# Attention scores in transposed form: 64x32 array tiles and VectorE's block transposes in place of TensorE's

## The chip, the cores and the metric

The kernel runs on one core of a Trainium2 chip. The metric is device time in microseconds (us), the median of several executions; lower is better. The core's engines work from queues of their own, each in program order: TensorE (PE, matmuls and transposes into PSUM), VectorE (DVE), ScalarE (ACT), GpSimd (POOL) and SyncE (SP), which issues most transfers.

## The reference

Three layers follow one another. The change is in the first, an attention whose 576 keys are first pooled into 32 memory slots a head (4 batches, 8 heads, 576 tokens, head size 64):

```python
a = softmax(phi)                      # over the 576 tokens, for each of 32 slots
k_m = einsum('bhsm,bhsd->bhmd', a, k) # 32 x 64 a head
v_m = einsum('bhsm,bhsd->bhmd', a, v)
scores = q @ k_m.T / sqrt(64)         # 576 x 32 a head
attn = softmax(scores)                # over the 32 slots
out = attn @ v_m                      # 576 x 64 a head
```

Its output, 2304 tokens by 512, goes through an ELU MLP (512 to 2048 to 512), and that through a mixture of 8 experts (512 to 1024 to 512, the best 2 of 8 for each token).

## The kernel before, in words

**Main loop.** Work is cut into units: four MLP blocks, one a batch of the attention in order (4, 5, 4, 5 tiles of 128 tokens, 16 steps each), then expert units of 8 steps. The loop (L914) runs over all steps; `i` counts them, so block 0 is i = 0 to 15, block 1 is 16 to 31, block 2 is 32 to 47. Each step issues, in this order: the top tick, a split of weights (`prep_hi` on ScalarE), the first layer (L781, two halves of 288 tokens in block units), the middle tick, the second half of the split, the ELU (ScalarE's two activations, L786 and L787, then VectorE's L794 and L795), in block 0 the conversion of packed weights (`conv1_hi`, `conv1_lo` on ScalarE, `conv2` on VectorE), the late tick, and the second layer of step i - 2 (L826 in block 0, L828 to L830 later). The first layer writes two PSUM banks `ph`, which come free when L795 has read them. So the first layer of step i + 1 follows VectorE's ELU of step i.

**Attention.** `attention(b)` (L139) is a generator. Batch 0 is run straight through before the loop, with an order written out by hand and filler matmuls (`warm`). Batches 1, 2 and 3 are put into blocks 0, 1 and 2: each `yield` names the kind of slot in which the next piece may run ("pe", "light", "gap"), and `tick` (L511) takes pieces at the top, in the middle and late in a step. By these rules the pieces of scores and softmax fall into i = 10 to 13 for batch 1, 25 to 29 for batch 2 and 39 to 43 for batch 3. The first layer of block b reads the result, `xt`, as a rounded high half and a low half (`th`, `tl`); the pooled values `vT` are multiplied into that layer's weights beforehand (`fold`, `fold_half`).

**Scores and softmax.** The pooled keys lie in `kmT`, 128 partitions (two heads, g = 0 and 1, of 64) by four pairs of heads, block-diagonal with zeros. `scores(k)` takes a group of two, two or one token chunks of 128 (the last of 64): a matmul a chunk and pair of heads (L256), whose stationary operand is the chunk of q, puts the tokens on partitions and 32 slots for each of 8 heads on the columns. VectorE takes the maximum over the slots (L269) and subtracts it (L270), out of PSUM; ScalarE takes the exponential (`grow`, L275); VectorE sums, adds 1e-9, inverts and multiplies (`normalize`, L281 to L285; for batch 0 GpSimd multiplies). `turn(k)` transposes back on TensorE (L292), into PSUM; ScalarE copies the rounded high half (L136) and VectorE subtracts for the low half (L137).

**PSUM.** Side work takes banks in turn from those that the second layer leaves free: `px`, and `acc4` too where the block has four tiles. In block 1 (five tiles) `px` is alone (`single()`), and the next piece waits until the last one's data have been read out.

## Time and profile before

| | |
|---|---|
| median of 3 runs | 922.81 us (922.67 to 923.54) |
| span of the profiled execution | 921.2 us |
| around the span, against the median | 1.6 us |
| busy: TensorE, VectorE, ScalarE, GpSimd | 885.3, 539.8, 441.1, 163.8 us |
| mean granted TensorE clock | 0.993 of full speed |
| attention of batch 0 | 0 to 28.3 us |
| block 0, with attention of batch 1 | 28.3 to 133.0 us |
| block 1, with batch 2 | 133.0 to 240.7 us |
| block 2, with batch 3 | 240.7 to 331.8 us |

The profile is of one execution and shows its span; the runs' times hold what lies around it too. Busy times are sums over the span; matmuls overlap one another and their ends are modelled. [...] In a timeline, brackets name the idle time before an instruction and what ended it.

### The profile page before, as it was taken

What the parts mean: (1) busy time and instruction counts of PE and PEld (TensorE: products, weight loads), DVE (VectorE), ACT (ScalarE), POOL (GpSimd) and SP (SyncE); (2) the same over time, 40 slices, a digit from 0 to 9 for tenths busy, and PEclk for the clock granted to TensorE, in tenths of its full rate; (3) what the DMA queues carried; (4) which work ended last, traced back from release to release, by engine and by line L of the source; (5) the groups of instructions that cost most, each with busy time, mean ns of one, the idle gap of its engine ahead of it and who ended that gap; (6) DMA issues with size and microseconds to landing.
All of it is one profiled execution on the core that took longest, in us unless ns stands there. A gap on an engine that the chain in (4) does not pass through costs nothing. (4 is left out here: it accounts for less than half of the span.)

```text
span 921.2 us, 15374 instructions
## 1 busy us (share of the span) xinstructions
PE 885.3 (96%) x5909; PEld 726.2 (79%) x5913; DVE 539.8 (59%) x1164; ACT 441.1 (48%) x967; POOL 163.8 (18%) x246
## 2 busy tenths in 40 slices
PE   8999899999999899999999999999999999999995
PEld 5556457777878777777888888898898998989884
DVE  4876877566687687458667564554544543443421
ACT  4776556445564655555546454443543343332310
POOL 1100000000000404210416412304404032030303
PEclk9999999999999999999999999999999999999998
DMA  9986568655652325441666966647647245162404
GB/s 344 398 292 234 178 229 307 199 200 160 241 180 92 93 92 139 138 138 58 182 153 155 264 206 193 165 133 223 162 155 180 82 97 163 46 147 92 57 1 57
DMA packets 67885, 152.62 MB, mean 166 GB/s; under 512 B 11106, under 2 KB 24162, under 8 KB 66786
## 3 DMA queue, kind: packets, MB, share of 16 engines
q1 hardware_dynamic: 57826, 131.13, 43.2%
q0 software_dynamic: 9984, 20.49, 11.8%
q8 instruction: 47, 0.77, 0.3%
q14 instruction: 28, 0.23, 0.1%
HBM read 119.16 MB, written 32.44 MB: 165 GB/s over the span
## 5 line engine op out<-in xcount | busy, mean ns | idle before, releaser
L828 PE MATMUL acc<-bh,gl 128*128 128x512 f32 (+1 forms) x544 | 217.5, 400 | 1.8 <-DVE rows L849 1.8
L830 PE MATMUL acc<-bh,gh 128*128 128x512 f32 (+1 forms) x544 | 213.7, 393 | 0.0
L829 PE MATMUL acc<-bl,gh 128*128 128x512 f32 (+1 forms) x544 | 213.5, 392 | 0.0
L809 DVE SCALAR_TENSOR_TENSOR gl<-ph,gh 128x312 fp32r<-128x312 f32 (+2 forms) x128 | 61.8, 483 | 217.9 <-ACT gh L808 217.9
L494 ACT ACTIVATE bh<-raw 128x512 fp32r<-128x512 f32 x144 | 90.1, 626 | 77.7 <-PE acc L830 77.6
L830 PEld LDWEIGHTS acc<-bh,gh 128*128 128x128 f32 (+1 forms) x544 | 101.4, 186 | 23.6
L828 PEld LDWEIGHTS acc<-bh,gl 128*128 128x128 f32 (+1 forms) x544 | 101.7, 187 | 19.8 <-DVE rows L849 2.2
L851 POOL DMA_INDIRECT out<-rows,ids x40 | 64.9, 1622 | 292.3 <-DVE rows L849 264.3
L829 PEld LDWEIGHTS acc<-bl,gh 128*128 128x128 f32 (+1 forms) x544 | 101.7, 187 | 18.0
L808 ACT ACTIVATE gh<-ph 128x312 fp32r<-128x312 f32 (+2 forms) x128 | 55.2, 431 | 124.5 <-PE ph L781 123.7
L500 DVE TENSOR_TENSOR bl<-raw,bh 128x512 fp32r<-128x512 f32 x144 | 98.8, 686 | 3.4 <-ACT bh L494 3.4
L781 PE MATMUL ph<-xl,ah 128*128 128x312 f32 (+2 forms) x512 | 96.9, 311 | 0.0
L781 PE MATMUL ph<-xh,ah 128*128 128x312 f32 (+2 forms) x512 | 94.3, 306 | 0.0
L781 PE MATMUL ph<-xh,al 128*128 128x312 f32 (+2 forms) x512 | 94.2, 306 | 0.0
L781 PEld LDWEIGHTS ph<-xl,ah 128*128 128x128 f32 x512 | 81.5, 188 | 6.5
L781 PEld LDWEIGHTS ph<-xh,al 128*128 128x128 f32 x512 | 79.4, 188 | 0.0
L781 PEld LDWEIGHTS ph<-xh,ah 128*128 128x128 f32 x512 | 79.4, 188 | 0.0
L781 PE MATMUL ph<-tl,fh 128*128 128x288 f32 x256 | 64.3, 332 | 4.9 <-DVE elu L795 4.6
L500 DVE TENSOR_TENSOR al<-raw,ah 128x512 fp32r<-128x512 f32 x96 | 65.6, 683 | 0.0
L781 PEld LDWEIGHTS ph<-tl,fh 128*128 128x128 f32 x256 | 41.1, 189 | 30.8 <-issue 14.3
L794 DVE SCALAR_TENSOR_TENSOR elu<-elu 128x288 f32<-128x288 f32 x128 | 57.8, 451 | 11.6 <-ACT elu L787 11.2
L801 ACT ACTIVATE gh<-elu 128x576 fp32r<-128x576 f32 (+1 forms) x48 | 31.8, 663 | 66.0 <-DVE elu L795 66.0
(214 smaller groups left out, 1247.4 us busy)
## 6 DMA issues: line engine op xcount, KB each, us to landing
raw<-in_wmoe SPq DMA_DIRECT2D x48, 1024.0 KB, 5.1
raw<-in_wmlp SPq DMA_DIRECT2D x32, 512.0 KB, 6.2
raw<-wxa SPq DMA_DIRECT2D x12, 1024.0 KB, 6.0
raw<-wxb SPq DMA_DIRECT2D x12, 1024.0 KB, 8.2
kv<-in_kv SPq DMA_DIRECT2D x8, 1024.0 KB, 10.6
out<-zrow SPq DMA_DIRECT2D x13, 512.0 KB, 9.1
q<-in_q SPq DMA_DIRECT2D x8, 576.0 KB, 7.5
x2d<-rows SPq DMA_DIRECT2D x18, 256.0 KB, 3.9
```

What stands on the lines that cost most here:

```text
L494: act.activation(ready[h, c][0], raws[h, c], AF.Copy)
L500: dve.tensor_tensor(lo, raws.pop((h, c)), hi.bitcast(F32), op=OP.subtract)
L781: pe.matmul(ph, w, x, start=k == 0, stop=k == len(terms) - 1)
L794: dve.scalar_tensor_tensor(m, t[:, 0, o], 1.0, m, op0=OP.add, op1=OP.mult)
L801: act.activation(gh[:, o], m, AF.Copy)
L808: act.activation(gh[:, o], ph, AF.Relu)
L809: dve.scalar_tensor_tensor(gl[:, o], ph, 0.0, gh[:, o].bitcast(F32), op0=OP.max, op1=OP.subtract)
L828: pe.matmul(acc, gl[:, o], wh, start=f == 0, stop=False)
L829: pe.matmul(acc, gh[:, o], wl, start=False, stop=False)
L830: pe.matmul(acc, gh[:, o], wh, start=False, stop=f == u["nf"] - 1)
L851: d = pool.indirect_dma_start(out=out, out_offset=bass.IndirectOffsetOnAxis(ap=ids[:m, t, 0:1], axis=0), in_=r, in_offset=None, compute_op ...
```

## The change

`kmT` keeps both heads g on the two halves of the partitions, without zeros, as one copy. `scores(h)` takes half of the tokens (288) and swaps the operands: `kmT` is the stationary operand, 64 rows by 32 columns, q the moving one. Four pairs of heads go to four column tiles and the two g to two row tiles, and the scores come out with 4 x 32 slots on partitions and 288 tokens on columns, one bank for each g. VectorE transposes 32x32 blocks out of PSUM into SBUF, which puts 32 tokens of a block on partitions and the slots on columns; maximum, subtraction, exponential and normalization then run over 128x288 pieces, one for each (h, g). A second block transpose on VectorE gives the layout of `xt`, ScalarE copies the high half from it, and `lower` subtracts the low half, one piece later in the order. Groups of three become quarters of four. In batch 0 the second half of the scores comes behind `fold_half(0)`, and `pooled([1])` ahead of the conversion; in batches 1 to 3 the kinds of slots change with the pieces.

```diff
--- before.py
+++ after.py
@@ -20,6 +20,7 @@
 
 P = 128
 NB, NH, S, HD, NM = 4, 8, 576, 64, 32
+H = S // 2
 N = NB * S
 DM, FF = 512, 2048
 NE, FE = 8, 1024
@@ -116,8 +117,7 @@
                 + [lambda h=h: load_q(b, h) for h in range(2)])
 
 
-    kmT = ap_.tile([P, 4, 2, NM], F32, tag="kmT", name="kmT")
-    dve.memset(kmT, 0.0)
+    kmT = ap_.tile([P, 4, NM], F32, tag="kmT", name="kmT")
     deferred, place = [], [""]
 
     def later(f):
@@ -215,9 +215,7 @@
 
             def put():
                 if 0 in ws:
-                    for g in range(2):
-                        o = slice(64 * g, 64 * g + 64)
-                        act.activation(kmT[o, :, g], bk[o, :P].rearrange("p (j m) -> p j m", m=NM), AF.Copy)
+                    act.activation(kmT.rearrange("p j m -> p (j m)"), bk[:, :P], AF.Copy)
                 if 1 in ws:
                     act.activation(vT, bk[:, P:2 * P], AF.Copy)
 
@@ -242,89 +240,80 @@
         yield
         qt = att["q", b]
         xt = att["x", b] = [fp.tile([P, 2, S], F32R, tag=n, name=n) for n in ("th", "tl")]
-        groups = [(0, 2, P), (2, 2, P), (4, 1, 64)]
         sbs = {}
 
-        def scores(k):
-            c0, k_, n = groups[k]
-            m = k_ * 8
-            bk = side_bank()
-            for i in range(k_):
-                s0 = SCH[c0 + i][0]
-                for p in range(4):
-
-                    pe.matmul(bk[:n, i * 256:(i + 1) * 256].rearrange("t (g j m) -> t j g m", g=2, j=4)[:, p],
-                              qt[:, p, s0:s0 + n], kmT[:, p], start=True, stop=True)
-            sc = bk[:n, :m * NM].rearrange("p (a b) -> p a b", b=NM)
-            mx = sm.tile([P, 16], F32, tag="smx", name="smx", bufs=2)
-            if k < 2:
-                sb = ap_.tile([P, 16, NM], F32, tag="sb", name="sb", bufs=2)
-            elif first:
-                sb = rp.tile([P, DM], F32, tag="rows", name="rows").rearrange("p (a b) -> p a b", b=NM)
-            else:
-                sb = aT[:, 0].rearrange("p a (b c) -> p (a b) c", c=NM)
-            sbs[k] = sb[:n, :m]
-
-            def shift():
-                dve.tensor_reduce(out=mx[:n, :m], in_=sc, axis=AX, op=OP.max)
-                dve.tensor_tensor(sbs[k], sc, mx[:n, :m, None].to_broadcast([n, m, NM]), op=OP.subtract)
-
-            later(shift)
-
-        def grow(k):
-            act.activation(sbs[k], sbs[k], AF.Exp, scale=0.125)
-
-        def normalize(k):
-            c0, k_, n = groups[k]
-            m, sb = k_ * 8, sbs[k]
-            su = sm.tile([P, 16], F32, tag="ssu", name="ssu", bufs=2)
-            dve.tensor_reduce(out=su[:n, :m], in_=sb, axis=AX, op=OP.add)
-            dve.tensor_scalar(su[:n, :m], su[:n, :m], 1e-9, None, op0=OP.add)
-            dve.reciprocal(su[:n, :m], su[:n, :m])
+        def scores(h, gs=(0, 1)):
+            bks = {g: side_bank()[:, :H] for g in gs}
+            for j in range(4):
+                for g in gs:
+                    o, r = slice(64 * g, 64 * g + 64), slice(32 * j, 32 * j + 32)
+                    pe.matmul(bks[g][r], kmT[o, j], qt[o, j, h * H:(h + 1) * H], start=True, stop=True,
+                              tile_position=(64 * g, 32 * j))
+
+            def shift(g):
+                sb = sbs[h, g] = ap_.tile([P, H // 32, NM], F32, tag="sb", name="sb", bufs=4)
+                mx = sm.tile([P, H // 32], F32, tag="smx", name="smx", bufs=2)
+                dve.transpose(sb.rearrange("p a b -> p (a b)"), bks[g])
+                dve.tensor_reduce(out=mx, in_=sb, axis=AX, op=OP.max)
+                dve.tensor_tensor(sb, sb, mx[:, :, None].to_broadcast([P, H // 32, NM]), op=OP.subtract)
+
+            for g in gs:
+                later(lambda g=g: shift(g))
+
+        def grow(h, g):
+            act.activation(sbs[h, g], sbs[h, g], AF.Exp, scale=0.125)
+
+        def normalize(h, g):
+            sb = sbs[h, g]
+            su = sm.tile([P, H // 32], F32, tag="ssu", name="ssu", bufs=2)
+            dve.tensor_reduce(out=su, in_=sb, axis=AX, op=OP.add)
+            dve.tensor_scalar(su, su, 1e-9, None, op0=OP.add)
+            dve.reciprocal(su, su)
             eng = pool if first else dve
-            eng.tensor_tensor(sb, sb, su[:n, :m, None].to_broadcast([n, m, NM]), op=OP.mult)
-
-        def turn(k):
-            c0, k_, n = groups[k]
-            bk = side_bank()
-            for i in range(k_):
-                for g in range(2):
-                    pe.transpose(bk[:, (i * 2 + g) * P:(i * 2 + g) * P + n],
-                                 sbs[k][:, i * 8 + g * 4:i * 8 + g * 4 + 4].rearrange("p a b -> p (a b)"),
-                                 ident[:n, :n])
-            s0 = SCH[c0][0]
-            src = bk[:, :k_ * 2 * P].rearrange("p (i g n) -> p g i n", i=k_, g=2)[:, :, :, :n]
-            later(lambda: halve(src, *(t[:, :, s0:s0 + k_ * n].rearrange("p g (i n) -> p g i n", i=k_)
-                                       for t in xt)))
+            eng.tensor_tensor(sb, sb, su[:, :, None].to_broadcast([P, H // 32, NM]), op=OP.mult)
+
+        def turn(h, g):
+            back = sbs[h, g, "back"] = ap_.tile([P, H], F32, tag="back", name="back", bufs=2)
+            dve.transpose(back, sbs[h, g].rearrange("p a b -> p (a b)"))
+            act.activation(xt[0][:, g, h * H:(h + 1) * H], back, AF.Copy)
+
+        def lower(h, g):
+            hi, lo = (t[:, g, h * H:(h + 1) * H] for t in xt)
+            dve.tensor_tensor(lo, sbs[h, g, "back"], hi.bitcast(F32), op=OP.subtract)
 
         if first:
             scores(0)
-            grow(0)
-            scores(1)
-            grow(1)
+            grow(0, 0)
+            grow(0, 1)
             warm(6)
+            pooled([1])
             conv2([("a", 0), ("a", 1)])
             load_to(3)
             keep([("a", 0), ("a", 1)])
             load_phi(1)
-            normalize(0)
-            pooled([1])
-            scores(2)
+            normalize(0, 0)
+            normalize(0, 1)
             conv1_hi(pieces(0))
-            grow(2)
             warm(6)
-            normalize(1)
             across([1])
+            turn(0, 0)
+            turn(0, 1)
+            lower(0, 0)
+            lower(0, 1)
             conv1_lo(pieces(0))
             warm(4)
-            turn(0)
-            normalize(2)
-            warm(2)
             fold_half(0)
             warm(2)
-            turn(1)
+            scores(1)
+            grow(1, 0)
+            grow(1, 1)
             warm(2)
-            turn(2)
+            normalize(1, 0)
+            normalize(1, 1)
+            turn(1, 0)
+            turn(1, 1)
+            lower(1, 0)
+            lower(1, 1)
             conv2(pieces(0))
             conv1_hi(pieces(1))
             conv1_lo(pieces(1))
@@ -332,29 +321,29 @@
                 f()
         else:
             yield "gap"
-            scores(0)
-            if single():
-                yield
-            scores(1)
+            for h in range(2):
+                if single():
+                    scores(h, [0])
+                    yield
+                    scores(h, [1])
+                else:
+                    scores(h)
+                yield "light"
+                grow(h, 0)
+                grow(h, 1)
+                if h == 0:
+                    yield
+            held = None
+            for h in range(2):
+                for g in range(2):
+                    yield "light"
+                    if held:
+                        lower(*held)
+                    normalize(h, g)
+                    turn(h, g)
+                    held = h, g
             yield "light"
-            grow(0)
-            grow(1)
-            yield
-            scores(2)
-            yield "light"
-            normalize(0)
-            grow(2)
-            yield "light"
-            normalize(1)
-            yield "gap" if b == 3 else "pe"
-            turn(0)
-            if single():
-                yield
-            turn(1)
-            yield "light"
-            normalize(2)
-            yield "gap"
-            turn(2)
+            lower(1, 1)
 
     def warm(n):
 
```

## Rows read from the trace of the kernel before

**Rows 1.** Page, first part: busy us (share of the span) and instructions of each engine.

```profile
PE 885.3 (96%) x5909; PEld 726.2 (79%) x5913; DVE 539.8 (59%) x1164; ACT 441.1 (48%) x967; POOL 163.8 (18%) x246
```

**Rows 2.** Windows in block 0 (us; busy us and instructions by engine; clock; DMA).

```profile
76.23:80.93 4.70, 4.70 (x23) 3.03 (x22) 3.73 (x6) 3.44 (x10) 0.00 (x0) 1.00 0.58 182
80.93:86.74 5.81, 5.81 (x38) 3.32 (x37) 4.30 (x9) 4.58 (x10) 0.00 (x0) 1.00 0.90 324
102.87:114.32 11.45, 7.96 (x31) 4.81 (x29) 9.92 (x18) 5.47 (x11) 0.00 (x0) 0.85 0.54 174
86.74:128.22 41.48, 36.87 (x201) 22.43 (x199) 33.44 (x57) 21.87 (x45) 0.00 (x0) 0.96 0.51 164
```

**Rows 3.** Waits of TensorE over the span: us in total, times, longest.

```profile
PE acc L292 <- DVE sb L285: 2.3, 1, 2.3
PE px L567 <- DVE tl L137: 2.0, 2, 1.0
```

**Rows 4.** Windows, end of block 3; the last columns are clock, DMA share, GB/s.

```profile
430.00:434.00 4.00, 4.00 (x16) 3.52 (x16) 3.21 (x8) 3.59 (x9) 0.00 (x0) 0.57 0.18 23
```

**Rows 5.** Windows in block 1: i = 23, and i = 24 to 30.

```profile
178.33:183.44 5.11, 5.11 (x31) 4.51 (x28) 3.75 (x8) 2.94 (x7) 0.00 (x0) 1.00 0.69 177
183.44:235.14 51.70, 48.83 (x376) 38.13 (x374) 33.72 (x76) 24.43 (x62) 0.00 (x0) 1.00 0.51 166
```

**Rows 6.** Windows in block 2: i = 40, and i = 39 to 43.

```profile
289.38:293.84 4.46, 4.46 (x26) 3.78 (x25) 3.44 (x8) 3.54 (x9) 0.00 (x0) 1.00 0.68 227
280.65:314.05 33.40, 30.95 (x236) 25.64 (x229) 27.23 (x61) 17.64 (x46) 4.19 (x10) 1.00 0.35 97
```

**Rows 7.** Groups by line, shapes apart: busy us, mean ns of one, idle before.

```profile
L256 PE MATMUL px<-kmT,q 128*128 128x64 f32 x64 | 7.7, 273 | 0.0
L794 DVE SCALAR_TENSOR_TENSOR elu<-elu 128x288 f32<-128x288 f32 x128 | 57.8, 451 | 11.6 <-ACT elu L787 11.2
L270 DVE TENSOR_TENSOR sb<-px,smx 128x512 f32<-128x512 f32 x4 | 2.8, 692 | 0.1
L285 POOL TENSOR_TENSOR sb<-sb,ssu 128x512 f32<-128x512 f32 x2 | 2.1, 1048 | 20.7 <-DVE ssu L283 20.7
```

**Rows 8.** Timeline of VectorE in block 2: start us, us, instruction.

```profile
306.74 0.40 DVE L281 TENSOR_REDUCE ssu<-aT 64x8 f32<-64x256 f32 x1
307.17 0.16 DVE L282 TENSOR_SCALAR ssu<-ssu 64x8 f32<-64x8 f32 x1
307.37 0.19 DVE L283 RECIPROCAL ssu<-ssu 64x8 f32<-64x8 f32 x1
307.60 0.42 DVE L285 TENSOR_TENSOR aT<-aT,ssu 64x256 f32<-64x256 f32 x1
307.94 0.17 DVE L671 TENSOR_TENSOR g_pr<-g_o,g_pos 128x32 f32<-128x32 f32 x1
```

**Rows 9.** Timeline of TensorE in blocks 1 and 3 (matmuls; idle before in brackets).

```profile
205.67 1.06 PE L419 MATMUL px<-raw,vT 64*32 64x512 f32 x8
206.66 0.53 PE L781 MATMUL ph<-tl,fh 128*128 128x288 f32 x2
...
429.33 0.54 PE L781 MATMUL ph<-tl,fh 128*128 128x288 f32 x2 [1.83 <-DVE elu L795]
```

**Rows 10.** Timeline of the start, all engines.

```profile
13.86 3.34 PE L256 MATMUL acc<-kmT,q 128*128 128x64 f32 x28 [0.19 <-DMA q<-in_q]
...
18.57 1.22 DVE L465 SCALAR_TENSOR_TENSOR cv<-cvm,cvl 128x1024 int32<-128x1024 int32 x1
...
23.86 1.24 ACT L457 ACTIVATE cvl<-raw,top 128x1024 int32<-128x1024 uint16 x1
...
28.32 0.54 PE L781 MATMUL ph<-tl,fh 128*128 128x288 f32 x2
...
31.31 0.46 DVE L794 SCALAR_TENSOR_TENSOR elu<-elu 128x288 f32<-128x288 f32 x1
...
32.31 0.53 PE L781 MATMUL ph<-tl,fh 128*128 128x288 f32 x2
```

## The prediction

> **What bounds the kernel now.** I read the page first: TensorE is busy for 96% of the span and no other engine for 60% [rows 1]. So work taken from TensorE is worth its time only where nothing else is late, and the windows by stretch say where that is. I cut the trace at the starts of the first layer (L781), one cut per iteration i of the main loop. In block 0 an iteration without attention work takes 4.70 us, and 5.81 us with a half fold in it, and VectorE is busy for 3.73 and 4.30 us of these [rows 2]: it has about a quarter to spare. While the softmax of batch 1 runs (i = 10 to 14) the same iterations take 41.48 us, and i = 12 alone 11.45 us, of which VectorE is busy for 9.92 [rows 2]. The list of waits shows the reason: TensorE stood 2.3 us in front of its transposes (L292) for VectorE's normalization (L285) [rows 3]. Block 1 runs at 5.11 us an iteration when undisturbed, with 3.75 us of VectorE, block 2 at 4.46 us with 3.44 [rows 5, 6]. The attention of batches 1, 2 and 3 is slipped into blocks 0, 1 and 2; that of batch 0 stands alone at the start. So the change acts in four places, and in three of them VectorE is nearly as full as TensorE. I sum up over the four.
>
> **What the pieces cost.** *TensorE, removed.* A batch has 20 score matmuls, two records each; 64 records of the full size cover 7.7 us, 0.12 us each [rows 7]. With the short last group that is 4.5 us a batch. Ten transposes at about the same pace add 1.2.
>
> *TensorE, added.* Sixteen matmuls of 64x32 tiles by 288 columns, eight for each half. The nearest rows are folds, which use the same tiles. Behind layer 1, a half fold of 256 columns lengthens an iteration by 5.81 - 4.70 = 1.1 us [rows 2]; at the top of an iteration a single-g fold of 512 columns takes 1.0 us from its start to the next layer 1 [rows 9], and 288 columns instead of 512 leave about 0.65. Both g together cost what one costs, since their tiles run side by side. So batches 1 and 3 pay about 1.1 + 0.65 each, batch 2, with one bank to itself and four separate sets, 0.65 + 3 x 1.1 = 3.95.
>
> *VectorE.* A 128x288 operation takes 0.45 us [rows 7]. In a chain, one that needs the last starts 0.43 us after a 0.40 us one, and one that doesn't starts 0.34 us after a 0.42 us one [rows 8]. For 288 columns I take 0.49 and 0.37. The four steps of a normalization start 0.43, 0.20, 0.23 and 0.34 apart at 256 columns [rows 8]. The block transpose isn't in the trace. Its bounds are the 256-wide reduction, 0.40 us [rows 8], and the 512-wide subtraction, 0.69 us [rows 7]; I take 0.48, nearest to the 288-wide row. [...]
> So one (h, g) quarter costs 1.34 us for transpose, maximum and subtraction, 1.75 for normalization and transpose back, 0.37 for the low half: 3.5 us, 14 a batch. Before, by the same spacings, it is 3.5 for the shifts, 4.8 for the normalizations, 1.5 for the low halves: 9.8. VectorE gets about 4.2 us more a batch.
>
> *ScalarE.* Four exponentials and four high halves of 288 columns against three and three wider ones: equal. But the high half (L136 before) is now issued right behind VectorE's transpose and ahead of ScalarE's elu activations of that iteration, so these now wait for VectorE's normalization too. The memset of kmT goes (once), and kmT takes one copy instead of two: 0.3 us at the start, not on the path, since the second load of q arrives at 13.86 us [rows 10].
>
> **Batch 0, at the start.** Scores of the first half are out at 14.5 us (q's arrival at 13.86, then two waves of tiles). VectorE: shifts to 17.4, the scale of the moved pooled([1]) at 18.2 (it follows that step's matmuls, estimate 1.8 us behind warm(6)), the two conversions to 20.7 (18.57 before [rows 10]), normalizations of both g to 22.4, GpSimd's products (0.66 us for 288 columns, from 1.05 for 512 [rows 7]) to 23.1, transposes, low halves to 24.5. The fold's halves wait for ScalarE's 1.24 us conversion (L457, at 23.86 before [rows 10]) and end at 26.3. Only then come the second half's shifts, behind them in VectorE's queue: 2.7 us, normalizations 1.9, the product 0.66, transpose, copy and low half 1.3: 32.8 us. Layer 1 of i = 0 starts its first half early (26.4, against 28.32 [rows 10]), but its second half needs these values and TensorE stands for about 5.7 us. Conversions of 2.4 us follow on VectorE before the elu (L794), which starts at 35.3 where it started at 31.31, so layer 1 of i = 1 goes from 32.31 [rows 10] to 36.3: 4.0 us lost. [...] Loss: 5.2.
>
> **Batch 1, i = 10 to 14 (41.48 us [rows 2]).** Times from layer 1 of i = 10. Both shifts (2.7 us) stand in front of elu: layer 1 of i = 11 at 6.6. In i = 11 the half fold needs the two banks of the second scores, and these come free only when VectorE has finished two conversions (2.5 us) and both transposes: TensorE stands 2.3 us, layer 1 of i = 12 at 15.4. At the top of i = 12 a normalization holds elu back: 21.2. Then a full VectorE turn: elu, two conversions, low half, normalization, transpose (end 26.6), the high half on ScalarE, low half, normalization, transpose (29.2), ScalarE's high half, elu: layer 1 of i = 13 ends at 22.9, that of i = 14 can't start before 31.1, that of i = 15 not before 39.4. Gain 2.1, less 0.7 in i = 15, whose elu waits for the conversions: 1.4. A low clock hides behind VectorE here.
>
> **Batch 2, i = 24 to 30 (51.70 us [rows 5]).** Seven times 5.11 is 35.8, four single folds 4.0, five gating pieces of four short instructions at 0.45 (pace of [rows 7]) 2.2: the attention part is 9.7. TensorE's waits for the bank px held by turn (2.0 us [rows 3]) are in it and go. After: 3.95 for the scores. In i = 28 to 30 VectorE has 4.2 us of quarters in each iteration beside its 3.75, so it falls behind: the fold at the top of i = 30 holds px until its ScalarE copy, queued behind the last high half, and its low half are done (44.4 us), and the gating transpose behind it, due at 41.7, stands 2.7 us. With a low clock in one of two cases (0.7) and one gating piece more inside the stretch, which i = 32 gets back, that is 7.4: gain 2.2.
>
> **Batch 3, i = 39 to 43 (33.40 us [rows 6]).** Times from layer 1 of i = 39. Layer 1 of i = 40 starts at 7.0 (8.73 before, the cut at 289.38 [rows 6]), of i = 41 at 12.6. From there each elu waits for two quarters (4.2 us with their ScalarE copies 0.4 each) beside VectorE's own 3.4: i = 42 at 18, 43 at 26.2, 44 at 33.9. Loss: 0.5.
>
> **Sum.** -5.2 + 1.4 + 2.2 - 0.5 = 2.1 us longer. The span shown is 921.2 us and the median 922.81; the 1.6 us around it stay, and I add the difference to the median: 924.9 us. After 315 us nothing changes.
> [...] By TensorE's bill alone (each iteration at its undisturbed length) the three batches would gain 24 us, 899.
>
> **Rivals.**
> *VectorE's queue closes up* (faster). If ScalarE's copies and the transposes interleave without holding elu, only VectorE's extra work counts: at the start it then ends 1.8 us later than now instead of 5.2, batch 1 gains 3.8 (8.0 of its 41.48 us are idle on VectorE, and 4.2 are filled), batch 2 4.6, batch 3 1.9: 922.8 - 8.5 = 914.3. For it: VectorE's idle time exists [rows 2, 6]. Against: both queues run in program order, and the dependent steps stand next to one another. It decides from a start that loses under 3 us. Chance 0.22.
> *The start costs half* (2.6 us), if the second half's chain overlaps the fold's: 922.3, no change. For it: the path there is the one I know least. Chance 0.22.
> *The transpose is dear* (slower still). At 0.69 us instead of 0.48, with about 21 of 32 transposes on the path, 4.4 us more: 929.3. Chance 0.14.
> The forecast itself, with its own range 923 to 928, has 0.42.
>
> **How the numbers follow.** 0.2%, 1.85 us, is what a measurement of this kernel tells from no change. Forecast and dear transposes are slower: 0.56; the half start is the same: 0.22; the closed queue faster: 0.22. The range reaches from 916, into the closed queue, to 930, the dear transpose.
>
> **What would show it.** L256's records shrink to 32 a batch and the transposes L292 are gone: TensorE's busy time falls. Layer 1 of i = 0 has its two halves apart by more than 5 us, and that of i = 1 starts near 36 to 38 us. VectorE's busy time rises by some 15 us; waits of layer 1 for elu (L795) grow in i = 13, 14 and 41 to 44; the gating transposes' wait in block 1 moves from tl to fl. I am wrong if layer 1 of i = 1 starts before 34, if a transpose takes under 0.4 us, or if the elu starts on time in i = 13 and 42.

## The result and the profile after

The changed kernel takes 934.21 us (median of 4 runs), the kernel before beside it 923.17: a ratio of 1.0124, 95% interval [1.0105, 1.0143], so 11.0 us longer where 2.1 were forecast. The direction was right; the time lies outside the range of 916 to 930.

Busy times of the page after, which answer to [rows 1]; some 16 us more on VectorE and 8 less on TensorE:

```profile
span 930.7 us, 15275 instructions
PE 877.7 (94%) x5835; PEld 710.3 (76%) x5839; DVE 555.7 (60%) x1222; ACT 439.6 (47%) x971; POOL 164.7 (18%) x247
```

The groups by shape show the new operations (busy, mean ns, idle before): a block transpose takes 0.47 to 0.48 us out of PSUM and out of SBUF alike.

```profile
L277 DVE STREAM_TRANSPOSE back<-sb 128x288 f32<-128x288 f32 x16 | 7.5, 471 | 1.4 <-POOL sb L273 1.0
L256 DVE STREAM_TRANSPOSE sb<-px 128x288 f32<-128x288 f32 x8 | 3.8, 480 | 2.2 <-PE px L250 2.0
L256 DVE STREAM_TRANSPOSE sb<-acc 128x288 f32<-128x288 f32 x8 | 3.8, 477 | 3.9 <-PE acc L250 2.8 <-PE px L250 1.1
```

I cut the trace after at the starts of the first layer (now L770), as that of before. The windows of batch 1, batch 2, i = 34 and 35, and batch 3; of before the first, second and last are in [rows 2, 5, 6]. A row gives the stretch, its length, the busy time and number of instructions of TensorE, its weight loads, VectorE, ScalarE and GpSimd, then the granted clock as a share of full speed, the share of the DMA engines and GB/s:

```profile
92.62:134.44 41.82, 33.95 (x182) 18.10 (x180) 34.83 (x70) 21.41 (x46) 0.00 (x0) 0.96 0.50 166
189.64:241.70 52.06, 47.81 (x362) 35.19 (x361) 37.89 (x91) 25.10 (x65) 0.00 (x0) 0.97 0.48 166
257.40:270.69 13.29, 11.27 (x73) 8.46 (x72) 12.01 (x34) 7.69 (x21) 0.00 (x0) 1.00 0.82 276
288.75:325.86 37.11, 30.23 (x219) 22.20 (x211) 31.46 (x77) 18.12 (x48) 5.41 (x12) 0.95 0.36 87
```

TensorE is busy for less time in each batch, and in this trace no batch is shorter. TensorE's longest waits, which answer to [rows 3] (total, times, longest):

```profile
PE ph L770 <- DVE elu L784: 8.5, 10, 1.8
PE ph L770 <- ACT fh L136: 6.0, 2, 4.3
PE ph L770 <- DVE tl L282: 5.7, 1, 5.7
PE px L556 <- DVE fl L137: 4.5, 3, 2.8
PE px L548 <- ACT x2T L558: 4.0, 2, 2.9
```

The waits for turn's transposes (L292) and for px behind tl are gone; these stand in their place. Where the difference arises, from the cuts of both traces (start of layer 1 after minus before; worked out, in us):

```
stage              before   after    adds
start, to i = 2     35.69    41.70   +6.0
batch 1, i = 10-15  46.21    46.72   +0.5
batch 2, i = 24-33  67.83    67.76   -0.1
i = 34 to 36        19.29    21.25   +2.0
batch 3, i = 39-43  33.40    37.11   +3.7
all, to i = 44                      +11.8
```

The other stages differ by under 0.2. Behind i = 44 the largest difference is one dip of the clock [rows 4] that the trace after lacks (1.4 us); the span is 9.5 us longer.

**The start.** TensorE's timeline, which answers to [rows 10]: the second half of layer 1 waits 5.66 us for the second half's softmax, then runs at a granted clock of 0.50, as do the fillers (L352) behind it, up to 37.6 us.

```profile
25.73 0.67 PE L770 MATMUL ph<-tl,fh 128*128 128x288 f32 x2 [1.76 <-ACT fh L136]
32.84 1.24 PE L770 MATMUL ph<-tl,fh 128*128 128x288 f32 x2 [5.66 <-DVE tl L282]
35.71 2.31 PE L352 MATMUL acc<-zrow,ones 128*128 128x512 bf16 x5 [0.22 <-issue]
38.66 0.53 PE L770 MATMUL ph<-tl,fh 128*128 128x288 f32 x2
```

The window from the end of that wait to layer 1 of i = 1; the granted clock, third number from the end, is 0.56:

```profile
32.80:38.60 5.80, 5.52 (x28) 2.75 (x29) 4.48 (x7) 3.75 (x8) 0.00 (x0) 0.56 0.65 215
```

**i = 13, batch 1.** VectorE's, ScalarE's and TensorE's timelines: the high half (L278) waits 2.35 us for VectorE's transpose and holds ScalarE's elu activations, VectorE then waits 1.11 us for these, and the half fold's copies (L136), which layer 1 of i = 14 waits for, come behind them. Layer 1 stands 4.26 us; VectorE is idle for 2.7 of the 11.78 us.

```profile
122.36 0.48 DVE L277 STREAM_TRANSPOSE back<-sb 128x288 f32<-128x288 f32 x1
122.88 0.44 ACT L278 ACTIVATE th<-back 128x288 fp32r<-128x288 f32 x1 [2.35 <-DVE back L277]
123.95 0.46 DVE L783 SCALAR_TENSOR_TENSOR elu<-elu 128x288 f32<-128x288 f32 x1 [1.11 <-ACT elu L776]
126.02 0.36 ACT L136 ACTIVATE fh<-acc 128x256 fp32r<-128x256 f32 x1
126.44 0.88 PE L770 MATMUL ph<-tl,fh 128*128 128x288 f32 x2 [4.26 <-ACT fh L136]
```

**i = 29, batch 2.** ScalarE's timeline: the high half (L278) has waited 2.35 us for VectorE's transpose, and the copy x2T, whose input was ready at 224, is queued behind it. On TensorE the gating matmul (L548) waits for that copy, and layer 2 then runs at one matmul every 0.43 us, at a granted clock of 0.52 (228.9 to 232.0), instead of 0.23.

```profile
227.50 0.44 ACT L278 ACTIVATE th<-back 128x288 fp32r<-128x288 f32 x1 [2.35 <-DVE back L277]
227.85 0.58 ACT L558 ACTIVATE x2T<-px 128x512 f32<-128x512 f32 x1
228.48 0.44 PE L548 MATMUL px<-wgs,x2T 128*32 128x16 f32 x32 [2.91 <-ACT x2T L558]
228.85 0.69 PE L817 MATMUL acc<-bh,gl 128*128 128x512 f32 x1
229.34 0.63 PE L818 MATMUL acc<-bl,gh 128*128 128x512 f32 x1
229.76 0.63 PE L819 MATMUL acc<-bh,gh 128*128 128x512 f32 x1
```

**i = 43, batch 3.** VectorE's, ScalarE's and TensorE's timelines: the fold's high half (L136) is queued behind the quarter's (L278), its low half (L137) behind the quarter, so px comes free at 320 and the gating transposes (L556) stand 2.81 us.

```profile
317.92 0.48 DVE L277 STREAM_TRANSPOSE back<-sb 128x288 f32<-128x288 f32 x1
318.43 0.44 ACT L278 ACTIVATE th<-back 128x288 fp32r<-128x288 f32 x1 [1.41 <-DVE back L277]
318.78 0.58 ACT L136 ACTIVATE fh<-px 128x512 fp32r<-128x512 f32 x1
319.39 0.69 DVE L137 TENSOR_TENSOR fl<-px,fh 128x512 fp32r<-128x512 f32 x1 [0.38 <-ACT fh L136]
320.14 0.66 PE L556 MATMUL px<-ident,rows 128*128 128x128 f32 x4 [2.81 <-DVE fl L137]
```

### The profile page after: what moved, and what is told of

It reads as the page before. It is cut to its first block, busy times and chain, and to the rows that moved or that the text cites. A ratio compares the mean times of both kernels' runs of the same rounds, so it can differ in the third digit from the quotient of the medians.

```text
span 930.7 us, 15275 instructions
## 1 busy us (share of the span) xinstructions
PE 877.7 (94%) x5835; PEld 710.3 (76%) x5839; DVE 555.7 (60%) x1222; ACT 439.6 (47%) x971; POOL 164.7 (18%) x247
## 5 line engine op out<-in xcount | busy, mean ns | idle before, releaser
L770 PE MATMUL ph<-xl,ah 128*128 128x312 f32 (+2 forms) x512 | 97.0, 311 | 0.0
L770 PE MATMUL ph<-xh,ah 128*128 128x312 f32 (+2 forms) x512 | 94.3, 306 | 0.0
L770 PE MATMUL ph<-xh,al 128*128 128x312 f32 (+2 forms) x512 | 94.2, 306 | 0.0
L770 PEld LDWEIGHTS ph<-xl,ah 128*128 128x128 f32 x512 | 81.5, 189 | 6.8 <-issue 0.3
L770 PE MATMUL ph<-tl,fh 128*128 128x288 f32 x256 | 65.0, 335 | 20.6 <-DVE elu L784 8.5
L770 PEld LDWEIGHTS ph<-tl,fh 128*128 128x128 f32 x256 | 41.5, 191 | 49.8 <-issue 14.9
L770 PEld LDWEIGHTS ph<-xh,al 128*128 128x128 f32 x512 | 79.4, 188 | 0.0
L770 PEld LDWEIGHTS ph<-xh,ah 128*128 128x128 f32 x512 | 79.3, 188 | 0.0
L783 DVE SCALAR_TENSOR_TENSOR elu<-elu 128x288 f32<-128x288 f32 x128 | 57.7, 451 | 11.4 <-ACT elu L776 11.1
## 6 DMA issues: line engine op xcount, KB each, us to landing
kv<-in_kv SPq DMA_DIRECT2D x8, 1024.0 KB, 10.4
```

The source lines that it names most:

```text
L770: pe.matmul(ph, w, x, start=k == 0, stop=k == len(terms) - 1)
L783: dve.scalar_tensor_tensor(m, t[:, 0, o], 1.0, m, op0=OP.add, op1=OP.mult)
```

## The experiments

Theory: the loss comes from where the new steps stand in the in-order queues of VectorE and ScalarE (queue theory), stage by stage (stage theory). Rivals: VectorE's added work as such (work theory), TensorE's clock after the waits, and stages that lean on one another. The table gives for each run the ratio to the kernel before on the same chip, and from its trace what each stage adds against the trace of before.

```
run                            ratio  [interval]        start  b.1   b.2  34-36  b.3  at i=44
changed kernel                 1.0124 [1.0105, 1.0143]  +5.9  +0.5  -0.1  +2.0  +3.7  +11.8
e1  only batch 0               1.0099 [1.0070, 1.0127]  +7.2  +0.9   0.0   0.0  -0.1   +7.9
e2  only batches 1-3           1.0064 [1.0039, 1.0089]  -0.3  +1.3  -0.1  +2.0  +2.1   +5.1
e3  scores(1) early            1.0100 [1.0074, 1.0127]  +4.2  +0.5  -0.2  +2.0  +3.7   +9.9
e4  high half later            1.0044 [1.0029, 1.0059]  +6.2  -2.9  -4.7  +2.0  +1.6   +2.1
e5  e4, start packed           0.9968 [0.9955, 0.9981]  +3.2  -2.9  -4.7  +1.9  +1.6   -0.9
e6  e4, old batch 0, gap       0.9963 [0.9935, 0.9990]  -0.1  -2.1  -4.7  (shifted)    -5.4
e7  transposed twice           1.0158 [1.0113, 1.0203]  +7.1  +3.2  +1.4  +2.0  +6.8  +20.4
e8  e4, transposed twice       1.0092 [1.0060, 1.0124]  +8.0   0.0  -2.8  +1.9  +2.1   +9.3
e9  e4, gating back            0.9996 [0.9973, 1.0018]  +7.9  -2.7  -4.7   0.0  +1.4   +1.8
e10 e9, old batch 0            0.9909 [0.9883, 0.9936]  -0.6  -2.6  -4.7   0.0  +1.4   -6.5
e11 e9, packed, products POOL  0.9896 [0.9870, 0.9922]  +2.5  -4.2  -5.4   0.0  -1.7   -9.0
e12 e11, old batch 0           0.9885 [0.9854, 0.9916]   0.0  -4.9  -5.4   0.0  -1.7  -12.2
e13 kernel before              (one run)                -0.3  -0.2   0.0   0.0  -0.1   -0.6
e14 changed kernel             1.0131 [1.0109, 1.0154]  +5.7  +1.7  -1.4  +2.0  +3.7  +11.6
e15 high half later            1.0040 [1.0023, 1.0056]  +6.4  -2.5  -4.7  +1.9  +1.6   +2.8
e16 packed start alone         1.0059 [1.0043, 1.0076]  +2.9  +1.6  -1.3  +1.9  +3.7   +8.8
```

"Start" is the difference at layer 1 of i = 10. The columns stop at i = 44 because on the chips of e5 to e12 that iteration itself took 11.4 to 13.9 us instead of 6.3; the runs of the kernel before were longer there too (medians of 935.9 instead of 921 us), but without a trace, so what they lost at i = 44 is not known.

The ratio is of medians and the stages are of one run, and the two do not always agree. The traced runs of e4 and e15 are the shortest and the second shortest of ten (921.45 and 921.49 us, medians 924.64 and 924.44), those of e14 and e16 the longest of four and five (936.40 and 931.58, medians 934.82 and 927.50). And the start alone, with the same order for batch 0, adds 5.7 to 8.0 us in the changed kernel, e4, e7 to e9, e14 and e15.

**One part alone: e1, e2.** Both paths in one kernel, a set of batches on the old one (with a block-diagonal kmT of its own, and on the new path one tile for both g of a half):

```diff
+        yield from (old_way() if b in OLD else new_way())   # e1: OLD = {1, 2, 3}; e2: OLD = {0}
```

> Batch 0 alone takes the new path, batches 1 to 3 keep TensorE's transposes. Stage theory (each stage's loss is its own, and what layer 1 loses at the start is not given back later): layer 1 of i = 1 starts at about 38.6 us instead of 32.3, and the whole is 5.5 to 6.5 us longer than before, about 929. Rival, VectorE's added work is paid for wherever it falls (15.9 us busy more, 11.0 us longer, so 0.7 us per us): a quarter of the work, 2.8 us longer, 926. Rival, the stages lean on one another (the late start is absorbed by slack in block 0 when batch 1 stays as it was): 0 to 2 us longer.

> Batch 0 keeps the old path, batches 1 to 3 take the new one. Stage theory: starts of layer 1 agree with before up to i = 9; batch 1 loses about 0.4 us, batch 2 nothing, the gating pieces at i = 34 and 35 2.0, batch 3 3.7: 4 to 6 us longer than before, about 928. Rival, VectorE's added work: three quarters of 11 us, 8.3 longer, 931.5. Rival, the stages lean on one another: with the start in time the batches come out even, 0 to 2 us longer.

The stages add up: e1 has the start's loss and nothing later gives it back, e2 the others, and +7.9 and +5.1 make 13.0 for 11.8. The leaning rival falls. e1's start is 1.3 us worse than the changed kernel's, and e1 as a whole longer than expected, but within the 5.7 to 8.0 us that this start takes.

e2 also prices the clock by chance: its i = 43 has the changed kernel's work and the same wait (2.80 us), but took 8.85 us instead of 10.45. The windows of that iteration, after and e2: TensorE's busy time and the length both differ by 1.6 us, and the clock by 0.16.

```profile
315.41:325.86 10.45, 7.64 (x65) 6.13 (x65) 8.09 (x23) 5.17 (x13) 5.41 (x12) 0.84 0.60 105
```

```profile
310.26:319.11 8.85, 6.05 (x64) 4.98 (x65) 7.90 (x22) 4.66 (x13) 4.03 (x10) 1.00 0.55 122
```

**The start's order: e3, e5, e16.** e3 moves the second half's scores and exponentials up:

```diff
             scores(0)
+            scores(1)
             grow(0, 0)
             grow(0, 1)
...
             pooled([1])
+            grow(1, 0)
+            grow(1, 1)
             conv2([("a", 0), ("a", 1)])
...
             fold_half(0)
-            warm(2)
-            scores(1)
-            grow(1, 0)
-            grow(1, 1)
-            warm(2)
+            warm(4)
             normalize(1, 0)
```

> The changed kernel with one move in batch 0: the scores of the second half, their shifts and exponentials come right behind those of the first half and ahead of the conversion, instead of behind the half fold. Queue theory (the start loses by where the second half stands in VectorE's queue): VectorE's 3.1 us of idle time between 14 and 35.7 us are filled, the elu of i = 0 starts at about 32.7 to 33.5 instead of 35.7, layer 1 of i = 1 at 35 to 36.5, the two halves of layer 1 of i = 0 are under 3 us apart, and the whole is 2.2 to 3.5 us shorter than the changed kernel. Rival, VectorE's work alone sets the start: elu within 0.7 us of 35.7 and the whole within 1 us of the changed kernel. Rival, low TensorE clock after the 5.7 us wait: as that wait goes, over 4 us shorter.

Layer 1 of i = 1 at 36.97 instead of 38.66, elu at 34.90 instead of 35.73: between the theories. VectorE's waits for GpSimd's products and ScalarE's copies had stayed. The packed start (e5 on top of e4, e16 alone) takes them out too (shortened: calls of one kind are put in words, and the lines that leave their old places are not shown):

```diff
+            scores(0), scores(1), grow of all four quarters
             warm(6)
             pooled([1])
             conv2([("a", 0), ("a", 1)])
+            normalize of all four quarters
             conv1_hi(pieces(0))
             warm(6)
             across([1])
+            warm(2)
+            fold_half(0)
             conv1_lo(pieces(0))
+            warm(14)
+            turn(0, 0), turn(0, 1), lower(0, 0), turn(1, 0), lower(0, 1), turn(1, 1), lower(1, 0), lower(1, 1)
             conv2(pieces(0))
```

> The kernel of the high half later, with one more change, in batch 0: both halves of the scores first, then the sums of all four quarters in front of GpSimd's four products, then fold and the four transposes, so that VectorE never stands behind GpSimd or ScalarE there. Queue theory for the start: the 3.1 us of VectorE's idle time that the changed kernel had there go, only VectorE's added work (about 1.8 us) is left: elu of i = 0 at 32.3 to 33 us, layer 1 of i = 1 at 33.5 to 35 instead of 38.7, and 3.5 to 5 us shorter than the kernel of the high half later. Rival, work: moving the scores alone gave 1.7 us at i = 1, and no order gives more: layer 1 of i = 1 not before 36.5.

> The changed kernel with the packed start of batch 0 alone, on the same chip as the changed kernel. Stage theory: layer 1 of i = 1 at 35 to 36 us instead of 38.7, the rest as in the changed kernel, 3 us shorter in the whole (0.3%). Rival, the late ScalarE copies that it leaves in batch 1 take the gain back by i = 15: under 1 us shorter.

Layer 1 of i = 1 at 35.88 and 35.69 us, in e5 between its theories (33.5 to 35, not before 36.5): half of the start's loss goes, 2.8 us on one chip (e14 against e16), and the batches behind it keep their times. So order made half of it; the other half stayed in every order that I tried. The medians of e14 and e16 are 7.3 us apart, and the traces up to i = 44 show only these 2.8; the rest is open.

**ScalarE's high half: e4.**

```diff
             dve.transpose(back, sbs[h, g].rearrange("p a b -> p (a b)"))
-            act.activation(xt[0][:, g, h * H:(h + 1) * H], back, AF.Copy)
...
                     yield "light"
                     if held:
-                        lower(*held)
+                        high(*held)          # the ScalarE copy of the quarter before
                     normalize(h, g)
                     turn(h, g)
+                    if held:
+                        lower(*held)
                     held = h, g
             yield "light"
+            high(1, 1)
             lower(1, 1)
```

> The changed kernel with one move in batches 1 to 3: ScalarE's copy of the high half of a quarter is issued at the head of the next piece instead of right behind VectorE's transpose, and the low half behind that next piece's transpose. Queue theory (ScalarE's copy waits for VectorE's transpose and holds the elu, the gating copy x2T and the fold's copies queued behind it): the waits of L548 for x2T (2.9 at i = 29) and of L421 go, batch 3 loses 1 to 2 us instead of 3.7, and the whole is 2 to 4 us shorter than the changed kernel. Rival, VectorE's work is what is late, whatever ScalarE does: within 0.7 us of the changed kernel, since VectorE's queue holds the same work.

> The changed kernel, unchanged, beside the kernel before and the next two on one chip. Stage theory: start +6, batch 1 +0.4, batch 2 0, i = 34 and 35 +2, batch 3 +3.7 as in its first profile, each within 0.5 us except the start, and 1.0 to 1.4% longer than before. If i = 44 is long it is so in both. Rival, part of the 11 us came from the chip of the first run: under 0.8%.

> The kernel of the high half later, unchanged, on the same chip as the changed kernel. Queue theory: 7 to 10 us shorter than the changed kernel at i = 44 (batch 1 2.9, batch 2 4.6, batch 3 2.1), and about 0.8 to 1% shorter in the whole. Rival, the difference between the first two chips made part of it: under 5 us.

This is the largest single part, and far more than the 2 to 4 us that I expected of e4 in the whole. On one chip e14 has 1.0131 and e15 1.0040, and at i = 44 they differ by 8.9 us: 4.1 in batch 1, 3.4 in batch 2, 2.1 in batch 3, less 0.8 that e15's start is worse. The rival that VectorE's work is late whatever ScalarE does falls. The edit moves VectorE's low half behind the next transpose as well, and no run has the two moves apart. At i = 29 of e4, ScalarE's timeline shows x2T ready early, behind a high half that waited 0.66 us, and TensorE does not stand:

```profile
220.60 0.44 ACT L282 ACTIVATE th<-back 128x288 fp32r<-128x288 f32 x1 [0.66 <-DVE back L277]
220.95 0.58 ACT L565 ACTIVATE x2T<-px 128x512 f32<-128x512 f32 x1
```

Its windows of batches 1, 2 and 3 have VectorE as busy as after, and shorter lengths:

```profile
92.89:131.47 38.58, 33.45 (x183) 18.05 (x181) 34.65 (x70) 21.28 (x46) 0.00 (x0) 0.96 0.53 177
186.65:234.10 47.45, 46.38 (x363) 33.99 (x361) 37.56 (x91) 24.65 (x65) 0.00 (x0) 1.00 0.53 181
281.14:316.14 35.00, 30.21 (x218) 22.14 (x211) 31.10 (x77) 17.90 (x48) 5.00 (x11) 0.95 0.29 94
```

Length less busy, VectorE's idle time falls from 7.0 to 3.9 us in batch 1, from 14.2 to 9.9 in batch 2, from 5.7 to 3.9 in batch 3. At i = 43 the move helps little: ScalarE's fold copy (L136) now starts at 308.02, but its subtraction (L137) stands behind the quarter in VectorE's queue until 309.69, the gating transposes still wait 2.34 us (2.81 after), and the clock still falls (0.83).

e14 repeats the first trace of the changed kernel except in i = 14 (9.3 us, not 8.0; the clock of batch 1 is 0.88, not 0.96), i = 29 (9.7, not 11.3, with the clock at 1.00, behind the same 2.91 us wait) and i = 11 and 12, whose sum is the same: some 1.5 us each way come and go with the clock. So 1.3 of the 4.1 us of batch 1 may be the clock's; against the first trace e4 gains 3.4 there.

**The price of VectorE's work: e7 (the changed kernel), e8 (e4).**

```diff
+            for _ in range(1 if first else 2):
                 dve.transpose(back, sbs[h, g].rearrange("p a b -> p (a b)"))
```

> The changed kernel with every back transpose of batches 1 to 3 done twice: 12 more instructions, about 0.43 us apart, 5.2 us of VectorE's time. It prices VectorE's work. Work theory (what VectorE gets more is paid in full): 4.5 to 5.5 us longer than the changed kernel. Queue theory (the elu and the copies behind the transposes wait, and VectorE is full only in some of the iterations): 2 to 4 us longer, nearly all of it in i = 13, 14, 29, 30, 42 and 43. If VectorE's idle time took it all: under 1 us.

> The kernel of the high half later with every back transpose of batches 1 to 3 done twice, the same 5.2 us of VectorE's time. Work theory: 4.5 to 5.5 us longer than the kernel of the high half later, as in the changed kernel. Queue theory (without ScalarE's copies in the way VectorE's idle time takes more of it): 1 to 3 us longer, less than in the changed kernel, most of it in batches 1 and 3, under 0.7 in batch 2.

The windows of e8's three batches are 5.3 us longer than e4's (2.9, 1.9, 0.5), those of e7 7.4 us longer than after's:

```profile
94.78:136.29 41.51, 34.82 (x183) 18.59 (x181) 37.44 (x75) 21.44 (x47) 0.00 (x0) 0.92 0.52 174
191.47:240.84 49.37, 46.41 (x363) 33.98 (x361) 39.39 (x95) 24.62 (x65) 0.00 (x0) 1.00 0.50 174
287.88:323.34 35.46, 28.61 (x218) 21.01 (x211) 32.75 (x79) 17.51 (x48) 3.78 (x8) 1.00 0.28 90
```

My queue theory said 1 to 3 and 2 to 4, so by the stages it fell as the whole story: VectorE's idle time took little of the work. In e8 it is 4.1, 10.0 and 2.7 us; only in batch 3 it is less than in e4, by 1.2 us. The split among the batches is not to be trusted, since the clock differs at i = 14 and at i = 43, which in the sum nearly cancels. The windows of these two, e4 and then e8:

```profile
123.63:131.47 7.84, 7.84 (x37) 4.58 (x37) 7.22 (x15) 4.42 (x9) 0.00 (x0) 0.81 0.47 144
306.17:316.14 9.97, 7.63 (x64) 6.12 (x65) 8.04 (x23) 5.49 (x14) 5.00 (x11) 0.83 0.44 119
```

```profile
127.08:136.29 9.21, 9.21 (x37) 5.11 (x37) 8.55 (x17) 4.65 (x10) 0.00 (x0) 0.67 0.53 168
314.44:323.34 8.90, 6.04 (x64) 4.97 (x65) 8.25 (x22) 5.11 (x14) 3.78 (x8) 1.00 0.42 120
```

In e7 the same two iterations have clocks of 0.67 and 0.72 where after has 0.79 and 0.84, and TensorE is busy for 2.3 us more in them, which leaves 5.1 of the 7.4 us. e8's ratio says the same as its stages, 4.4 us more than e4; e7's ratio is only some 3 us above the changed kernel's, from another chip, and does not bear out its stages. So in these stages the length is VectorE's work, paid about one for one (5.3 us in e8 for the 5.2 added), plus an idle time that the order sets; e4 cuts the second, and what cuts the first should gain as well.

**The gating pieces: e6, e9.** In the changed kernel quarters take slots of the kind "light" where transposes took "pe". So gating(0) gets ahead by one slot: its light pieces run in i = 32 to 35, not 33 to 36. Two ways to move them apart, batch 3 later (e6) and the gating back (e9):

```diff
-        for _ in range(0 if first else 4 if b == 1 else 2):
+        for _ in range(0 if first else 4 if b == 1 else 2 if b == 2 else 3):   # e6, with batch 0 on the old path
```

```diff
         u, z, ln, r = tmp("u"), tmp("w"), tmp("ln"), tmp("r")
+        if blk == 0:
+            yield "gap"                                                        # e9
         yield "light"
```

> Batch 0 on the old path, batches 1 to 3 on the new one with the high half later, and batch 3 started one slot later (three gaps instead of two), so that its maximum over phi does not meet the row copies and gating pieces of i = 34 and 35. Stage theory: i = 0 to 9 as before, batch 1 gains 2.5 to 3, batch 2 4 to 5, i = 34 and 35 lose under 0.7 us instead of 2.0, batch 3 loses 0 to 2: 4 to 7 us shorter than before, about 916 to 919. Rival, the two us of i = 34 and 35 are lost wherever the gating pieces fall: still 2.0 there. Rival, the stages lean on one another and the start's delay had been hidden in what batch 1 gained: 0 to 2 us shorter than before.

> The kernel of the high half later, with the gating of block 0 held back by one gap, so that its light pieces stand in the same iterations (33 to 36) as in the kernel before; in the changed kernel they stand one slot earlier (32 to 35), because a quarter's slot is of another kind than a transpose's. Gating theory: i = 34 and 35 take 5.4 and 5.9 us as before, not 6.2 and 7.1, i = 36 stays at 8.0, and the whole is 2 us shorter than the kernel of the high half later. Rival, VectorE's queue is behind at i = 34 and 35 for another reason (batch 2's end): i = 34 and 35 stay at 6.2 and 7.1. The batches and the start stay as they were.

In e6 i = 34 is as before, but i = 35 takes 8.35 us and the pieces of batch 3 land elsewhere; it shows only a shift. e9 is plain: 5.43 and 5.86 us, the two of before, where after has 6.19 and 7.10. The windows of i = 34 and 35, after and then e9: VectorE has 3 and 2 instructions fewer in them.

```profile
257.40:263.59 6.19, 5.51 (x41) 3.83 (x39) 5.94 (x17) 2.50 (x7) 0.00 (x0) 1.00 0.76 252
263.59:270.69 7.10, 5.76 (x32) 4.63 (x33) 6.07 (x18) 5.19 (x14) 0.00 (x0) 1.00 0.88 298
```

```profile
251.69:257.12 5.43, 5.43 (x41) 3.83 (x39) 4.99 (x14) 2.49 (x7) 0.00 (x0) 1.00 0.89 299
257.12:262.98 5.86, 5.48 (x40) 4.69 (x32) 5.62 (x16) 4.98 (x13) 0.00 (x0) 1.00 0.88 319
```

**Put together: e10, e11, e12.** e10 is e9 with batch 0 on the old path. e11 has all batches on the new path, the packed start, and GpSimd for the products of batches 1 to 3, with the transpose a piece later; e12 is e11 with batch 0 on the old path.

```diff
-            eng = pool if first else dve
-            eng.tensor_tensor(sb, sb, su[:, :, None].to_broadcast([P, H // 32, NM]), op=OP.mult)
+            pool.tensor_tensor(sb, sb, su[:, :, None].to_broadcast([P, H // 32, NM]), op=OP.mult)
...
+            parts = [(h, g) for h in range(2) for g in range(2)]
+            for n in range(6):
+                yield "light"
+                if n > 1:
+                    high(*parts[n - 2])
+                if n < 4:
+                    normalize(*parts[n])
+                if 0 < n < 5:
+                    turn(*parts[n - 1])
+                if n > 1:
+                    lower(*parts[n - 2])
```

> Batch 0 on the old path, batches 1 to 3 on the new one with the high half later, the gating of block 0 held back by one gap. Stage theory: starts agree with before up to i = 9, batch 1 gains 2.2 to 2.9 us, batch 2 4.7, i = 34 and 35 nothing, batch 3 loses 1.6: 5.3 to 6 us shorter than before at i = 44, 0.6% in the whole. Rival, VectorE's added work is paid in full (some 11 us in the three batches, less the 11.2 of TensorE's that are saved): within 1 us of before.

> All batches on the new path: batch 0 with the packed start, batches 1 to 3 with the high half later, GpSimd instead of VectorE for the twelve products of the normalizations (the back transpose moves one piece later), and the gating of block 0 held back. VectorE's work falls by 12 x 0.37 = 4.4 us. Work theory (in these stages one us of VectorE's time costs one us, as the doubled transposes cost 5.3 in the kernel of the high half later): start 3.1 lost, batch 1 gains 4 to 5, batch 2 5 to 6, batch 3 gains 0 to 1: 6 to 8 us shorter than before at i = 44. Rival, queue theory alone (only waiting of one queue for another costs, VectorE's work is free): as the kernel of the packed start with the gating held back, 3 us shorter than before. Rival, GpSimd's 0.67 us products and its own wait come back as waits of VectorE: longer than that.

> Batch 0 on the old path, the rest as in the kernel with GpSimd's products. Work theory: 3 us shorter than that kernel (the start), 9 to 11 us shorter than before at i = 44. Queue theory alone: as the kernel with the old batch 0 and the gating held back, 5 to 6 us shorter than before.

All three are faster than the kernel before: 0.9909, 0.9896 and 0.9885, and the stages up to i = 44 say so too (6.5, 9.0 and 12.2 us). That is somewhat more than the work theory said (6 to 8 for e11, 9 to 11 for e12), and twice or three times what waiting alone would give (3, and 5 to 6). None of the three ran on a chip with the short i = 44. With the products on GpSimd (0.74 us each, mean of twelve) batch 3 turns from 1.4 lost to 1.7 gained. e12's windows of the three batches: VectorE's work has shrunk by 1.2 to 2.0 us against e4's, and its idle time is 3.5, 10.4 and 2.6.

```profile
86.77:123.16 36.39, 31.89 (x183) 16.73 (x181) 32.94 (x66) 20.83 (x46) 2.69 (x4) 1.00 0.56 187
178.34:225.10 46.76, 46.19 (x363) 33.99 (x361) 36.40 (x87) 24.75 (x65) 3.70 (x7) 1.00 0.54 184
270.19:301.85 31.66, 27.35 (x218) 20.90 (x211) 29.11 (x70) 16.69 (x45) 6.90 (x13) 1.00 0.33 101
```

**The kernel before once more: e13.**

> The kernel before, unchanged, with a profile from the chip that the next three share. In five profiles from two other chips, all of experiments, the iteration i = 44 took 11 to 14 us instead of 6.3, with ScalarE, VectorE and TensorE idle together. Chip theory (it is not the change): on such a chip the kernel before shows it too, its span is 7 us or more longer than 921, and the stages up to i = 43 agree with the profile before within 0.5 us. Rival, the new code brings it: i = 44 takes 6.3 us here while the changed kernel beside it takes 12 or more.

Its chip was one without the long i = 44 (6.2 to 6.3 us in e13 to e16), so the question of the long i = 44, which is in all eight traces of e5 to e12, was not decided; the stages agree with the first trace of before within 0.3 us. What stops the engines there on two chips stays open.

## Why the prediction was wrong

The mechanism that the prediction forecast is there, VectorE fuller and TensorE waiting for it, but each of its four terms came out worse than sized and a fifth was left out. At i = 44 the sum of -2.1 is -11.8: the start misses by 0.8 us, batch 1 by 1.9, batch 2 by 2.1, i = 34 and 35 by 2.0, batch 3 by 3.2.

**Right.** The costs of the operations: 0.48 us a transpose (so the dear one falls), VectorE 15.9 us busier (15 said). Both g of a half together cost what one costs: from the first score matmul (L250) to TensorE's next work it is 0.65 us with both (at 94.69) and 0.62 with one (at 195.30) (about 0.65 said for 288 columns). None of the three signs under "I am wrong if" came, so they did not guard against this miss. The start's mechanism: the second half waits 5.66 us (5.7 said), elu starts at 35.73 (35.3). Batch 3 up to the start of layer 1 of i = 43: 7.4, 13.0, 18.2 and 26.7 us behind i = 39, where the prediction had 7.0, 12.6, 18 and 26.2. Batch 1 up to i = 12: 6.6 and 15.4, as said.

**Start, sized at -5.2: -6.0.** The elu is 4.4 us later than before (4.0 said), and layer 1 of i = 1 6.4 us (5.2 said). The 1.2 us by which the 5.2 exceed the 4.0 are a term that no run shows; in their place the trace has 1.9 us, behind fillers at a granted clock of 0.50 (32.8 to 37.6). In other runs of the same order the start costs up to 8.0.

**Batch 1, sized at +1.4: -0.5, and -1.7 in e14.** The failing step is i = 13, "the high half on ScalarE, low half, normalization, transpose, ScalarE's high half, elu": it was named, but the iteration took 11.8 us where I had 9.9. I had counted VectorE as continuously full there, and it stood idle for 2.7 us of the iteration and 7.0 of the stage, waiting for ScalarE's copies and activations, which stand behind its own transposes. i = 12 took 0.9 us more than the 5.8 that I had; i = 14 and 15 gave 0.8 back. e15 takes 4.1 us out against e14, on one chip.

**Batch 2, sized at +2.2: 0.1, and 1.4 in e14.** The step "the fold at the top of i = 30 holds px until its ScalarE copy" put the stall one iteration late and on the wrong tile. What stood behind ScalarE's high half was the gating's copy x2T at i = 29: 2.9 us, and 1.6 more by the clock (0.52 behind the wait; 1.00 and no such loss in e14), for which I had put 0.7, a term that no run shows. That the stall's length was as forecast (2.7) is luck. Nothing in the step asked what else ScalarE has queued there. In e14, without that clock, the gain is still 1.5 us less than my terms give, which no run traces to a step. The sign "the gating transposes' wait in block 1 moves from tl to fl" was wrong with it: in block 1 the wait is for x2T, and the one for fl is in block 2.

**i = 34 and 35, not in the sum: -2.0.** I saw "one gating piece more inside the stretch" of batch 2 and gave its time back in i = 32. I did not follow the pieces behind it, which all run one slot sooner and meet the row copies and batch 3's maximum over phi. e9 undoes it and the 2.0 us go.

**Batch 3, sized at -0.5: -3.7.** Nearly all of the miss is i = 43: the gating transposes wait 2.8 us for px, held by a fold whose halves are queued behind the quarter's, above all in VectorE's queue (e4 leaves 2.3 of it), and the clock falls, which costs 1.6 us. I had costed the elu alone.

**The rivals.** *VectorE's queue closes up* describes e4 in batch 2 (4.7 gained, 4.6 said) and, less 0.9, batch 1 (2.9, 3.8 said), not the start and not batch 3. It needed an order that the change does not have. *The start costs half* is e5. TensorE is busy 7.6 us less in the changed kernel, and that is 11.0 longer. In e10 three of four batches have the same matmuls and transposes, in another order, and the kernel is faster than before (0.9909), so in these batches most of the loss was the order's.

## What to carry to other kernels

When an engine hands a step to another in the same piece of work, look at all that is queued behind the receiver's instruction: here moving a 0.44 us ScalarE copy from right behind VectorE's transpose to the head of the next piece, and the subtraction that needs it to that piece's end, gave 9 us. Where an engine has no slack, price both its work and the idle time that the order forces on it; only the sum tells the length of the stage. After pieces change their kind or number, follow the other generators' pieces through the slots, up to the end, not only within the stretch.

## What was not expected of the hardware

A wait of TensorE can cost again behind it, and not every time: after 2.8 us of standing at i = 43 the clock of the iteration was 0.84 in one run and 1.00 in another (e2) with the same work, 10.45 and 8.85 us; e3, e14 and e16 took 10.44 to 10.47. Behind the 5.66 us wait at the start it was 0.56 for 5.8 us. A 128x288 fp32 block transpose costs VectorE 0.48 us out of PSUM and 0.47 out of SBUF, about what a subtraction of that shape costs (0.46).
